# Plain float32 attention scores with a bias row for heads 8 to 11 of an attention, gate and spatial-mixing kernel

## The chip, the core and the metric

The kernel runs on one core of one Trainium2 chip. The metric is the device time of one execution in microseconds (us). The core's engines work side by side, each through its own list of instructions in order: PE (TensorE, matmuls; its weight loads are listed as PEld), DVE (VectorE), ACT (ScalarE), POOL (GpSimd) and SP (SyncE, which here only issues DMAs). An instruction that waits holds up all that stands behind it on its engine.

## What is computed

Three layers follow each other for a batch of 4 with 576 positions. The first is causal attention with 8 heads of width 64 (32 heads over the batch), whose scores get a bias from running sums of `s`; the second is a gated linear layer whose gate is a causal convolution over five positions; the third is a mixing layer over positions.

```python
scores = scale * np.matmul(q, k.transpose(0, 1, 3, 2))
s_pos = np.maximum(s, 0.0)
cum = np.cumsum(s_pos, axis=-1)
bias = -(cum[:, :, :, None] - cum[:, :, None, :])
scores = np.where(causal, -1000000000.0, scores + np.minimum(bias, 0.0))
scores = scores - np.max(scores, axis=-1, keepdims=True)
attn = np.exp(scores)
attn = attn / (np.sum(attn, axis=-1, keepdims=True) + 1e-09)
...
return np.matmul(attn, v).astype(np.float32)
...
gate = 1.0 / (1.0 + np.exp(-gate_pre))
val = x @ w_val
return (gate * val @ w_out).astype(np.float32)
...
h = np.maximum(x @ w_in, 0.0)
u, v = (h[..., :d_ff // 2], h[..., d_ff // 2:])
v_n = (v - mu) / np.sqrt(var + 1e-06)
v_s = np.einsum('ts,bsd->btd', w_spatial, v_n) + b_spatial[None, :, None]
gated = u * v_s
return (gated @ w_out).astype(np.float32)
```

The part of the bias that depends on the row alone drops out of the softmax, so a head's scores are q times k, plus the running sum of the column, under the causal mask.

## The kernel before

The main loop runs over heads, `w` from 0 to 32. In round `w` the kernel emits the scores of head `w` (`scores`), the transposes of head `w - 1` (`transposes`), and in every second round the product with v for a pair of heads (`pv`) and their convolution (`conv`). A head's queries are cut into five tiles of 64, 128, 128, 128 and 128 rows; their causal widths in keys are 64, 192, 320, 448 and 576, and the last is done as two pieces of 288 columns. That makes six score products of 1600 columns together per head.

There are two ways to a head's scores, chosen by `h < NATIVE`:

- **Native** (heads 1 to 7; head 0 likewise, but adds the sums by a second matmul): `load` brings q and k in float32 to 64 partitions of a buffer `raw` (two of them, `raw0_66` and `raw1_67` in the listings below, used in turn), and a row of running sums to partition 64, where the q side has ones. `scores` then issues one float32 matmul per product (L214), straight from `raw`.
- **Split** (heads 8 to 31): `load` brings q and k twice, to 128 partitions. `prep` rounds them on ACT (`hi_of`, L72, tile `qk`), subtracts on DVE (`lo_of`, L79, tiles `qk` and `kd`), and copies the rounded q by DMA to `cn` (L171); the running sums, split in two rows, come by DMA to `kd` (L169). `scores` then issues two matmuls in the rounded format per product (L216 and L217).

`load(w + 2)` is issued at the start of round `w` when `w >= NATIVE` and at its end otherwise. A native head's `raw` buffer is read by PE until the head's last score product; a split head's buffer is free once `prep` has read it.

Between these pieces `more` takes steps from a queue of other work and lets them in by an amount `n_g` per round: while heads run, the queue folds two weight matrices into one (`fold_prep`, `fold`: L420 to L422 from `wih`, `wil`, `wo_h`, results `wch` and `wcl`), prepares weights that arrive as float64 (`weight_prep`: load L380, ACT L382 and L388, DVE, a split, store L412 to `wv_d` or `wo_d`), and does the later layers of the batch before (`mixing_a`, `mixing_b`). In `mixing_a` the gate needs a sigmoid over the finished convolution `z` (L514), for which ACT loads another table and then returns to that of the exponential. `mixing_b` begins with four products read out by ACT at L544 and a fifth read out at L549, and its PSUM tiles `psm` are two in number, so a third product waits until the first is read out.

The row sums of a pair of heads travel from ACT to DRAM (L247, `r_d`) and back to a broadcast tile `R` (L253); DVE's L305 multiplies the pair's output by it.

The order in which each engine's instructions stand is not fixed by hand: the framework schedules the emitted pieces with a timeline of its own, so a change in one place can move others.

Of the kernel before, what the change touches and what calls it, by code (L numbers as in the profile page):

```python
# [13 lines left out]
PSUM = bass.MemoryType.PSUM  # L14

NEG = -1.0e30
NATIVE = 8


F64_LOW = 2.0 ** (896 // 8 - 127 + 16)  # L20
# [4 lines left out]
def tile_stickbreak_attention_moe(  # L25
# [52 lines left out]
    def lo_of(eng, out_, in_, hi):  # L78
        eng.tensor_tensor(out=out_, in0=in_, in1=f(hi), op=ALU.subtract)  # L79
# [51 lines left out]
    cum_d = dram.tile([NH, 2, S], F32, name="cum_d")  # L131
    one_d = dram.tile([max(NATIVE, 1), S], F32, name="one_d")

# [5 lines left out]
    def load(h, cum=None):  # L139
        if h >= NH:  # L140
            return
        raw[h] = r = RAW[h % 2]
        src = qk2[h].rearrange("p (t s) -> p t s", t=2)
        if h < NATIVE:
            SY.dma_start(r[0:64], src[0:64])
            if h:
                if h < 3:
                    SY.dma_start(r[64:65, 0, :], f(cn[0][64:65]))
                SY.dma_start(r[64:65, 1, :], one_d[h:h + 1] if cum is None else cum[h:h + 1])
        else:  # L150
            SY.dma_start(r, src)
        vraw[h] = early.tile([128, 5, D], F32, tag="vraw", name="vraw", bufs=4)
        SY.dma_start(vraw[h], vp[h].rearrange("p (c d) -> p c d", c=5))
# [3 lines left out]
    def prep(h):  # L157
# [3 lines left out]
        r = raw.pop(h)  # L161
        if h < NATIVE:
            st[h] = r
# [27 lines left out]
    def scores(h, tiles):  # L191
        if h >= NATIVE:
            qa, kb, qc, kd = st[h]
# [7 lines left out]
        for i in tiles:  # L201
            q0, m, e = QS[i], QM[i], QE[i]
            spans = [(0, e)] if e <= 512 else [(0, HS), (HS, e)]
            for a, b in spans:
                if pst is None or o + b - a > 512 or len(spans) > 1:
                    pst = room("s", "pss", h)
                    o = 0
                if h < NATIVE:
                    r = st[h]
# [128 lines left out]
    lo_of(V, cl, cum, ch)  # L338
    if NATIVE:
        load(0, cum)  # L340
# [446 lines left out]
```

## Time and profile before

| | |
|---|---|
| time, median of 3 runs | 522.56 us (522.26 to 524.95) |
| span of the profiled execution, from its first to its last instruction | 522.8 us |
| mean granted TensorE clock, as a share of full speed | 0.977 |
| PE busy | 491.1 us, 94% of the span |
| PEld busy | 414.2 us, 79% |
| ACT busy | 340.7 us, 65% |
| DVE busy | 316.6 us, 61% |
| POOL busy | 125.9 us, 24% |

The profiled execution's own time is given only as its span. Shares are averages over stages with different limits; matmuls are pipelined and their ends are modelled, so "busy" on PE is not the same as work at full pace.

### The profile page before, as it was taken

To read this page: it belongs to the slowest core of one execution; us is meant where nothing else is said; L and a number is where in the kernel's file an instruction comes from. 1 tells how busy PE (TensorE), PEld (TensorE's weight loads), DVE (VectorE), ACT (ScalarE), POOL (GpSimd) and SP (SyncE) were. 2 spreads that over 40 slices of the span, in tenths; PEclk is the share of its full clock that TensorE was granted. 3 is DMA by queue.
4 is the path that set the end of the run, shared out by engine and by line. 5 is a ranking of instruction groups with operands and counts; after the bars stand their busy time and mean duration, and the time that the engine had idled before them with its cause. 6 is when DMAs were issued, how large, how long until landed. Compare 5 with 4: busy or idle time off the path is not lost.

```text
span 522.8 us, 9120 instructions
## 1 busy us (share of the span) xinstructions
PE 491.1 (94%) x3206; PEld 414.2 (79%) x3206; DVE 316.6 (61%) x836; ACT 340.7 (65%) x819; POOL 125.9 (24%) x166
## 2 busy tenths in 40 slices
PE   7988888889997999989999999999998999999997
PEld 4555555769786898978958889888878888998997
DVE  5697999597986784834648456743876525025120
ACT  3797897697848783875738647795869644224322
POOL 5131221014452013201333013003233013145140
PEclk8699999998998999999999999999998999999999
DMA  6746964455572452266521302666510061700002
GB/s 180 240 134 212 300 245 147 119 168 189 175 242 92 132 184 82 64 216 204 178 83 39 127 27 84 192 211 178 169 32 15 26 209 70 241 1 1 1 3 89
DMA packets 28335, 69.27 MB, mean 132 GB/s; under 512 B 4033, under 2 KB 12385, under 8 KB 28289
## 3 DMA queue, kind: packets, MB, share of 16 engines
q1 hardware_dynamic: 23360, 63.88, 39.3%
q10 hardware_dynamic: 4928, 4.80, 2.7%
q8 instruction: 25, 0.41, 0.3%
q14 instruction: 22, 0.17, 0.1%
HBM read 55.96 MB, written 9.16 MB: 125 GB/s over the span
## 4 chain that ended last, share of the span: by engine, by line
PE 64%; DMA 12%; ACT 10%; DVE 9%; issue 3%; POOL 1%; SPq 1%; ACTq 0%; DVEq 0%; POOLq 0%
PE psm L420 12%; PE psm L422 11%; PE psm L421 11%; PE pst L276 6%; PE pso L300 5%; PE psm L592 3%; PE psm L594 3%; PE psm L593 3%; PE pss L216 3%; ACT p L229 2%; DVE z L317 2%; PE pss L217 2%; DMA R<-r_d 2%; DMA wo_d<-wr 2%; DVE p L224 1%
## 5 line engine op out<-in xcount | busy, mean ns | idle before, releaser
L229 ACT ACTIVATE p<-p,nm 64x64 f32<-64x64 f32 (+4 forms) x160 | 88.7, 556 | 15.2 <-DVE nm L224 14.7
L276 PE MATMUL pst<-ident,p 128*128 128x128 f32 x480 | 81.6, 279 | 6.2 <-ACT p L229 3.6
L224 DVE CUSTOM_DVE_ANT_0 p<-pss,mask 64x64 f32<-64x64 f32 (+4 forms) x160 | 63.9, 419 | 25.8 <-PE pss L217 19.2
L277 ACT ACTIVATE pt<-pst 128x512 f32<-128x512 f32 (+1 forms) x128 | 61.5, 497 | 26.3 <-PE psq L300 15.6
L276 PEld LDWEIGHTS pst<-ident,p 128*128 128x128 f32 x480 | 59.1, 142 | 17.4 <-ACT p L229 4.6
L317 DVE SCALAR_TENSOR_TENSOR z<-x,cw,z 128x575 f32<-128x575 f32 (+1 forms) x64 | 57.6, 901 | 6.2 <-ACT z L314 5.8
L79 POOL TENSOR_TENSOR y<-gt,y 128x288 fp32r<-128x288 f32 x32 | 27.4, 861 | 106.7 <-ACT y L72 106.7
L79 POOL TENSOR_TENSOR g<-gt,g 128x288 fp32r<-128x288 f32 x32 | 28.7, 901 | 101.1 <-ACT g L72 101.0
L300 PE MATMUL pso<-pt,vraw 128*64 128x448 f32 (+3 forms) x320 | 46.8, 418 | 0.6 <-ACT pt L277 0.6
L216 PE MATMUL pss<-qk 128*64 128x64 f32 (+1 forms) x144 | 44.9, 330 | 0.6 <-DVE qk L79 0.5
L217 PE MATMUL pss<-kd,cn 66*64 66x64 f32 (+1 forms) x144 | 41.9, 296 | 0.0
L300 PEld LDWEIGHTS pso<-pt,vraw 128*64 128x64 f32 x320 | 22.0, 136 | 24.9 <-issue 18.0
L420 PE MATMUL psm<-g,wch 128*128 128x288 f32 x128 | 39.7, 312 | 0.2 <-DVE v L550 0.2
L497 DVE TENSOR_TENSOR gt<-psm,u 128x288 f32<-128x288 f32 x32 | 14.4, 456 | 40.6 <-PE psm L596 30.4
L592 PE MATMUL psm<-wsh,vh 128*128 128x288 f32 x128 | 38.4, 305 | 0.6 <-DVE gt L497 0.6
L421 PE MATMUL psm<-g,wcl 128*128 128x288 f32 x128 | 38.7, 302 | 0.0
L422 PE MATMUL psm<-g,wch 128*128 128x288 f32 x128 | 38.3, 301 | 0.0
L593 PE MATMUL psm<-wsh,vl 128*128 128x288 f32 x128 | 37.5, 298 | 0.0
L594 PE MATMUL psm<-wsl,vh 128*128 128x288 f32 x128 | 37.4, 297 | 0.0
L497 DVE TENSOR_TENSOR gt<-psm,z 128x288 f32<-128x288 f32 x32 | 14.3, 451 | 34.7 <-PE psm L422 32.6
L214 PE MATMUL pss<-raw 128*128 128x288 f32 (+4 forms) x84 | 28.3, 438 | 6.3 <-DVE nm L224 6.2
L72 ACT ACTIVATE y<-gt 128x288 fp32r<-128x288 f32 x32 | 14.0, 442 | 29.2 <-DVE gt L497 29.2
(171 smaller groups left out, 1358.1 us busy)
## 6 DMA issues: line engine op xcount, KB each, us to landing
raw<-in_qk SPq DMA_DIRECT2D x24, 576.0 KB
wv<-wv_d SPq DMA_DIRECT2D x12, 512.0 KB
wv<-wo_d SPq DMA_DIRECT2D x12, 512.0 KB
vraw<-in_vp SPq DMA_DIRECT2D x32, 160.0 KB
R<-r_d SPq DMA_DIRECT2D x32, 160.0 KB
out<-ot ACTq DMA_DIRECT2D x32, 144.0 KB
cn<-qk SPq DMA_DIRECT2D x24, 144.0 KB
wr<-in_w_in SPq DMA_DIRECT2D x5, 512.0 KB
```

What stands on the lines that cost most here:

```text
L79: eng.tensor_tensor(out=out_, in0=in_, in1=f(hi), op=ALU.subtract)
L216: T.matmul(pst[0:m, o:o + b - a], qa[:, q0:q0 + m], kb[:, a:b], start=True, stop=False)
L224: LAST["V"] = V.tensor_tensor_reduce(out=p[i][0:m, a:b], in0=src, in1=mask[0:m, o:o + b - a], scale=-0.125, scalar=3.0e38 if a == 0 else n ...
L229: A.activation(p[i][0:m, 0:e], p[i][0:m, 0:e], AF.Exp, bias=nm[0:m, i:i + 1], scale=-1.0, accum_out=sm[h // 2 % 2][0:m, h % 2, i:i + 1])
L276: T.transpose(pt[:, o - o0:o - o0 + 128], p[i][:, c * 128:(c + 1) * 128], ident[:, r:r + 128])
L277: A.activation(PT[h][:, o0:end], pt[:, 0:end - o0], AF.Copy)
L300: m = T.matmul(po[64 * j:64 * j + 64, a - q0:q1 - q0], vs[j][:, c, :], pts[j][:, o:o + q1 - a], start=c == cs[0], stop=c == cs[-1])
L317: V.scalar_tensor_tensor(out=z[:, d:], in0=x[:, :S - d], scalar=cw[:, p, k:k + 1], in1=z[:, d:], op0=ALU.mult, op1=ALU.add)
L420: T.matmul(pt, ah, bh, start=j == 0, stop=False)
L421: T.matmul(pt, al, bh, start=False, stop=False)
L422: T.matmul(pt, ah, bl, start=False, stop=j == n - 1)
L592: T.matmul(o, vh[c][:, cs], wsh[:, c, hs[hf]], start=c == 0, stop=False)
```

## The change

One number changes. Heads 8 to 11 go the native way.

```diff
-NATIVE = 8
+NATIVE = 12
```

What follows from it in the code: for these four heads `prep` only hands `raw` on, so two ACT roundings, two DVE subtractions and two DMAs (`cn`, `kd`) per head are not issued; `load` brings 64 partitions in place of 128, and one more row from `one_d` (which holds 12 rows in place of 8); the six products of a head are one float32 matmul each in place of a pair; and `load(10)` to `load(13)` are issued at the end of rounds 8 to 11 and not at their start. On PE, the order from head 23 on is the same as before.

Three places show how the order moves. Numbers behind an underscore tell buffers and tiles apart, and those of the tiles differ between the two programs for the same tile.

The first is ACT around the end of head 8 (`p04`) and the beginning of head 9 (`p10`, `p11`). `rt` are the row sums of heads 6 and 7. Before:

```order
L277 ACTIVATE pt_820<-pst_874 128x512
L229 ACTIVATE p03_109,sm0_102<-p03_109,nm_810 128x448
L72 ACTIVATE qk_996<-raw0_66 128x576 x2
L229 ACTIVATE p04_110,sm0_102<-p04_110,nm_810 128x576
L229 ACTIVATE p10_117,sm0_102<-p10_117,nm_934 64x64
L229 ACTIVATE p11_118,sm0_102<-p11_118,nm_934 128x192
L246 ACTIVATE rt_832<-psr_830 10x128
L247 DMA r_d_131<-rt_832 10x128
```

The same place in the changed kernel:

```order
L229 ACTIVATE p03_109,sm0_102<-p03_109,nm_802 128x448
L257 ACTIVATE wch_63<-psm_899 128x512
L246 ACTIVATE rt_822<-psr_820 10x128
L277 ACTIVATE pt_810<-pst_855 128x512
L229 ACTIVATE p04_110,sm0_102<-p04_110,nm_802 128x576
L247 DMA r_d_131<-rt_822 10x128
L229 ACTIVATE p10_117,sm0_102<-p10_117,nm_914 64x64
L229 ACTIVATE p11_118,sm0_102<-p11_118,nm_914 128x192
```

The DMA of the row sums moves ahead of head 9's first two exponentials, and head 10's two roundings, which stood ahead of it, are gone.

The second is ACT ahead of `mixing_b`'s fifth read-out (L549). `wr` is the last of the four chunks of `w_out2` to be prepared, which arrives by DMA. Before:

```order
L72 ACTIVATE vh0_1346<-v_1263 128x512
L544 ACTIVATE v_1421<-psm_1420 128x512
L72 ACTIVATE vh1_1416<-v_1351 128x512
L544 ACTIVATE v_1473<-psm_1472 128x512
L277 ACTIVATE pt_1684<-pst_1688 128x512
L277 ACTIVATE pt_1684<-pst_1721 128x512
L229 ACTIVATE p12_119,sm0_102<-p12_119,nm_1674 128x320
L388 ACTIVATE wr_1932<-wr_1932 128x512
L549 ACTIVATE v_1559<-psm_1558 64x512
```

The same place in the changed kernel:

```order
L544 ACTIVATE v_1372<-psm_1371 128x512
L72 ACTIVATE vh0_1299<-v_1221 128x512
L72 ACTIVATE vh1_1367<-v_1304 128x512
L277 ACTIVATE pt_1460<-pst_1464 128x512
L544 ACTIVATE v_1425<-psm_1424 128x512
L277 ACTIVATE pt_1460<-pst_1498 128x512
L388 ACTIVATE wr_1884<-wr_1884 128x512
L229 ACTIVATE p03_109,sm0_102<-p03_109,nm_1450 128x448
L549 ACTIVATE v_1511<-psm_1510 64x512
```

L388, which waits for the chunk's DMA, stands close ahead of L549 in both. The chunk's buffer is the one that the second chunk's store has to leave; from the second chunk's rounding on ACT to this L388 there stand 12 instructions before the change, two of them L544, and 16 after it, four of them L544.

The third is SP's queue around the load of head 13. Before, it stands among heads 10 to 12's preparation, well ahead of all chunks of `w_out2`:

```order
L153 DMA vraw_932<-in_vp 128x320
L169 DMA kd1_99<-cum_d_134 2x576
L171 DMA cn1_97<-qk_1170 64x576
L151 DMA raw1_67<-in_qk2 128x1152
L169 DMA kd0_98<-cum_d_134 2x576
L253 DMA R_1232<-r_d_131 64x640
L482 DMA wv_1146<-wv_d_132 128x1024
```

In the changed kernel the load of head 13 is the first of the two `raw1_67` here, behind the store of the first chunk of `w_out2`:

```order
L380 DMA wr_1762<-in_w_out2 128x1024
L447 DMA wsr_1731<-in_wsT 128x576
L153 DMA vraw_1217<-in_vp 128x320
L153 DMA vraw_1402<-in_vp 128x320
L412 DMA wo_d_133<-wr_1719 128x1024
L151 DMA raw1_67<-in_qk2 128x1152
L380 DMA wr_1820<-in_w_out2 128x1024
L482 DMA wv_2293<-wo_d_133 128x1024
L171 DMA cn1_97<-qk_1491 64x576
```

Its buffer is now one that head 11's last score product on PE has to leave, and the load of the third chunk, `wr_1820`, stands behind it. On ACT, head 13's roundings (`qk_1491`), the second chunk's rounding, the third chunk's L388 and the first L544 follow each other directly in the changed kernel.

## Rows read from the trace of the kernel before

**Rows 1.** The page's busy time of each engine in us, share, instructions.

```profile
PE 491.1 (94%) x3206; PEld 414.2 (79%) x3206; DVE 316.6 (61%) x836; ACT 340.7 (65%) x819; POOL 125.9 (24%) x166
```

**Rows 2.** Busy time by stretch of the span; the first column is the stretch.

```profile
core 0: us, PE busy (x) PEld busy (x) DVE busy (x) ACT busy (x) POOL busy (x), PEclk, DMA share, GB/s
78.10:99.40 21.30, 18.95 (x115) 14.35 (x116) 15.90 (x41) 15.03 (x39) 1.72 (x1) 1.00 0.46 146
99.40:118.40 19.00, 14.79 (x102) 11.34 (x101) 17.86 (x49) 17.27 (x37) 2.46 (x2) 1.00 0.51 151
118.40:121.90 3.50, 3.50 (x17) 3.50 (x16) 1.10 (x3) 3.50 (x10) 1.57 (x2) 0.51 0.84 318
121.90:159.40 37.50, 34.55 (x214) 29.29 (x212) 31.60 (x73) 25.32 (x62) 16.76 (x19) 1.00 0.59 186
159.40:162.80 3.40, 3.32 (x8) 2.65 (x9) 2.78 (x10) 3.38 (x8) 2.74 (x3) 0.50 0.00 0
162.80:296.10 133.30, 131.08 (x915) 115.45 (x914) 84.26 (x222) 91.26 (x225) 28.54 (x33) 1.00 0.41 128
```

**Rows 3.** Timeline of PE: start, us, what; in brackets idle before, releaser.

```profile
84.04 0.74 PE L422 MATMUL psm<-wil,wo_h 128*128 128x512 f32 x2 [0.58 <-DVE wil L79]
...
87.36 0.33 PE L276 MATMUL pst<-ident,p 128*128 128x128 f32 x1 [1.05 <-ACT pt L277]
...
89.36 0.97 PE L300 MATMUL pso<-pt,vraw 128*64 128x448 f32 x4 [0.62 <-ACT pt L277]
...
101.96 0.50 PE L420 MATMUL psm<-wih,wo_h 128*128 128x512 f32 x1 [1.94 <-DVE wcl L79]
...
116.82 0.87 PE L276 MATMUL pst<-ident,p 128*128 128x128 f32 x6 [1.76 <-ACT p L229]
...
159.48 0.80 PE L420 MATMUL psm<-wih,wo_h 128*128 128x512 f32 x1 [2.73 <-DVE v L550]
```

**Rows 4.** Timeline of PE where it does not wait: the pace of products.

```profile
74.00 1.14 PE L214 MATMUL pss<-raw 128*128 128x288 f32 x4
74.97 0.27 PE L276 MATMUL pst<-ident,p 128*128 128x128 f32 x1
...
97.62 0.40 PE L422 MATMUL psm<-wil,wo_h 128*128 128x512 f32 x1
97.86 0.29 PE L216 MATMUL pss<-qk 128*128 128x288 f32 x1
...
98.39 0.27 PE L276 MATMUL pst<-ident,p 128*128 128x128 f32 x1
```

**Rows 5.** Groups by line and shape: count, then busy us, mean ns, idle before.

```profile
L72 ACT ACTIVATE qk<-raw 128x576 fp32r<-128x576 f32 x48 | 30.1, 676 | 3.7 <-PE pss L216 3.5 <-DMA raw<-in_qk 0.2
...
L79 DVE TENSOR_TENSOR kd<-raw,qk 64x576 fp32r<-64x576 f32 x24 | 19.6, 818 | 0.5
...
L79 DVE TENSOR_TENSOR qk<-raw,qk 64x576 fp32r<-64x576 f32 x24 | 18.8, 783 | 6.0 <-ACT qk L72 5.3
```

**Rows 6.** Timelines of ACT's queue, SP's queue and DVE: heads 6 and 7's row sums.

```profile
92.87 0.28 ACTq L247 DMA_DIRECT2D r_d<-rt  x1
...
96.39 1.11 SPq L253 DMA_DIRECT2D R<-r_d  x2
...
100.42 0.62 DVE L305 TENSOR_TENSOR x<-pso,R 128x448 f32<-128x448 f32 x1 [1.63 <-DMA R<-r_d]
```

**Rows 7.** The chain that ended last: start, us, what; the end of weight preparation.

```profile
145.68 8.11 DMA wo_d<-wr
...
153.81 3.55 DMA wr<-in_w_out
```

**Rows 8.** Timeline of ACT: the sigmoid of the first batch, and the fourth chunk's L388.

```profile
112.46 2.13 ACT L514 ACTIVATE z<-z 128x2304 f32<-128x2304 f32 x1
...
157.44 0.65 ACT L388 ACTIVATE wr<-wr 128x512 int32<-128x512 uint32 x1 [3.43 <-DMA wr<-in_w_out]
```

## The prediction

> **What bounds the kernel now.** I read the page's busy time first, then cut the span into stretches, then went through PE's timeline for the places where it waits, and last followed the longest of these waits back through the chain. The page puts PE at 94% of the span and its weight loads at 79% [rows 1]; no other engine is near. But this is an average. By stretch [rows 2], PE's idle time is the length less the busy time: 21.30 - 18.95 = 2.35 us from 78.1 to 99.4 (heads 8 and 9), 19.00 - 14.79 = 4.21 us from 99.4 to 118.4, 37.50 - 34.55 = 2.95 us from 121.9 to 159.4, together 9.5 us; and then only 133.30 - 131.08 = 2.2 us in the next 133 us. So the heads that the change touches run in the one part where PE still waits for others, and behind it PE is simply full. In the two short stretches at 118.4 and 159.4 the granted clock is 0.51 and 0.50, that is 1.2 GHz in place of 2.4; right before them PE had waited 1.76 us (the wait at 116.82) and 2.73 us [rows 3]. Work of 3.5 and 3.4 us at half clock loses half of it: 1.75 and 1.7 us.
>
> The waits themselves [rows 3] are for ACT and DVE being late: 0.58, 1.05 and 0.62 us in head 8; 1.94 us at 101.96 for DVE's L79, which stood behind a product that waited for the broadcast row sums [rows 6]; 1.76 us at 116.82 for ACT, which had done the sigmoid's 2.13 us and the table loads around it [rows 8]; and 2.73 us at 159.48 for DVE's L550, which hangs on ACT's L549, which stood behind an L388 that waited 3.43 us for its weights [rows 8].
>
> PE's busy time also hides short gaps, since a matmul's modelled end overlaps the next one. Weight loads show them better: they are busy 115.45 / 133.30 = 87% of the full stretch, and (14.35 + 11.34 + 29.29) / 77.80 = 71% of the three stretches that wait [rows 2]. At 87% these 54.98 us of loads would take 63.5 us, so there are 14.3 us to spare, 4.8 us more than the idle time shows. The Trainium skill, in "Perfetto Trace Analysis", section Identifying the Most-Contended Engine, calls matmul busy time a poor measure and gives weight-load occupancy as a better one. By that rule the 94% would be no ground to charge each added PE microsecond to the span; by the busy figure alone it would be. The trace agrees with the rule as far as 71% against 87% goes.
>
> **The change part by part.**
>
> *More PE work.* Two native products of 288 columns took 74.97 - 74.00 = 0.97 us in their four records, 0.485 us each. Two split pairs of 288 columns took 98.39 - 97.86 = 0.53 us, 0.265 us each [rows 4]. The difference is 0.22 us per 288 columns; a head has 1600 columns, so 0.22 x 1600 / 288 = 1.22 us, and four heads cost **+4.9 us** of PE time. If it fell only into waits it would cost 0; I charge all of it and count the waits that go as gains of their own.
>
> *Less ACT and DVE work.* Eight roundings at 676 ns are 5.4 us of ACT; four pairs of subtractions at 818 and 783 ns are 6.4 us of DVE [rows 5]. Neither is worth its length: both engines are waited for only at the places above. What is late next is what counts:
>
> - Head 8's three waits, 2.25 us. Ahead of them both engines lose heads 8 and 9's conversion, 2.7 us of ACT and 3.2 us of DVE by the same means. More than the waits; but PE's own scores take 1.2 us longer there and ACT has other work. I take **-2.0 us** (between 0 and 2.25).
> - The wait of 1.94 us at 101.96. The DMA of the row sums was issued on ACT at 92.87, the broadcast on SP at 96.39, and DVE's product started at 100.42 after 1.63 us of idling [rows 6]. In the new order that DMA stands ahead of head 9's first two exponentials, and two roundings (1.35 us) ahead of it are gone [rows 5]; with head 8's 2 us this is earlier by more than 1.94 us, and SP has no `cn` copy left ahead of the broadcast. I take **-1.9 us** (0 to 1.94).
> - The sigmoid's wait of 1.76 us and the half clock behind it, 1.75 us. The sigmoid, its two table loads and what they hold up stay. It moves to an earlier place among ACT's instructions, and PE can do no more mixing than two PSUM tiles until it is done. I take 0 (0 to -3.5).
> - The wait of 2.73 us at 159.48 and its 1.7 us of half clock. The chunk's load waits for the second chunk's store; these took 8.11 and 3.55 us [rows 7]. This time runs from the second chunk's rounding. Before, 12 instructions of ACT cover it, two of them L544; afterwards 16, four of them L544. An L544 comes after twelve products of 512 columns, 97.86 - 97.62 = 0.24 us each [rows 4], so 2.9 us of PE; two more cover 5.8 us against a wait of 3.43 us [rows 8]. I leave 0.5 us of the wait and take **-3.9 us** (0 to -4.4).
> - Short gaps, 4.8 us at most by the weight loads: with ACT and DVE lighter by 5 to 6 us some go; a fifth, **-1.0 us** (0 to -4.8).
>
> *A new wait.* Head 13's load now needs `raw1` from head 11's last product, and the third chunk's load stands behind it on SP. On ACT, head 13's roundings and the third chunk's L388 stand right ahead of the first L544, and PE can do two products of four weight chunks each (24 matmuls, 5.8 us) and some transposes before it needs that L544. The load is 576 KB; at the 3.55 us that 512 KB took [rows 7] it is 4.0 us, and with two roundings (1.35 us) some 5.4 us are gone before the split and the L388. If the third chunk's load lands beside it, PE waits next to nothing, 0.3 us; if it follows, 3.55 us more, 3.9 us. ACT's wait then also holds head 12's exponentials. I take **+1.0 us**, nearer the low end, since the DMA engines are half idle there (share 0.59) [rows 2] and two loads can run side by side.
>
> *At nothing:* the halves of the four loads that fall away, the four `cn` copies and the `kd` rows, and the four new rows of running sums. They ran beside other work, at a DMA share of about half [rows 2]; no PE wait above ends on one of them.
>
> Sum: 4.9 - 2.0 - 1.9 - 3.9 - 1.0 + 1.0 = **-2.9 us**, on the profiled 522.8 us a span of 519.9 us. That execution stands 0.2 us from the median, 522.56 us, so I forecast a time of **519.7 us**.
>
> **The rivals.**
>
> 1. *The sigmoid's wait goes too.* With PE's list heavier there, and the convolution done sooner, the stall may shrink under other work and the clock stay at 2.4 GHz: 3.5 us more, and with half of the short gaps 1.4 more, 514.8 us. For it: the broadcast that fed the last convolution comes earlier. Against: ACT's stall of 2.13 us and two table loads is the same length. The Trainium skill, in "TensorE: Matmul & The Clock Gate", section What's actually happening, says the slow clock is the default state that activity releases; by that rule a fuller PE would keep 2.4 GHz. The trace agrees in that both half-clock stretches follow PE's longer waits, but a wait of 1.94 us was followed by none.
> 2. *The last wait stays.* The weights come when the DMAs bring them, and the mixing that needs them comes earlier. Then the 3.9 us are not got back: 519.7 + 3.9 = 523.6 us, no change. For it: 8.11 us of store and 3.55 us of load in a row [rows 7], which no compute engine shortens.
> 3. *Slower: PE's work counts in full and the new wait takes the gain's place.* If head 13's load and the third chunk's follow each other, PE stands at the third product with the full 3.9 us, and drops to half clock as at 159.4, 1.7 us: 519.7 + 2.9 + 1.7 = 524.3 us; with the last wait kept as well, 528.2 us; with a part of it, 526. It decides the sign when the new wait and its clock cost more than 2.9 + 1.0 = 3.9 us. For it: nothing but those loads stands between head 11's last product and the L544. Against: the share of idle DMA time.
>
> That the change does not do what it says is not to be expected: in the new lists the four heads' pairs are gone.
>
> **How the numbers follow.** My forecast, with 516.5 to 521.5 us as its own range, gets 0.45; the first rival 0.18, the second 0.19, the third 0.18. A change of 0.5%, 2.6 us, is about what a measurement of this kernel can tell from none; so faster means below 519.95 us, slower above 525.2 us. Faster: 0.6 of the forecast's 0.45 and all of the first rival's 0.18, 0.45. Same: the other 0.18 of the forecast, 0.16 of the second rival, 0.06 of the third, 0.40. Slower: 0.15. The range runs from 514.0 us (most of the first rival) to 526.0 us (most of the third).
>
> **What would show it.** Right: PE starts head 10 about 1 to 2 us sooner than 99.4, no wait near 1.94 us for L79 in head 9, and no half clock ahead of L549's product; the wait of DVE for `R` there is gone. PE's added time shows as four L214 heads at about 2.7 us each. Wrong: an L388 wait of over 3 us ahead of L544 or L549, with PE idle and a half-clock stretch behind it; or a sigmoid that stalls PE for longer than 1.8 us; or new PE waits after 163 us, where there were none of weight.

## The result and the profile after

The changed kernel took 528.93 us (median of 4 runs, 525.65 to 530.26) against 522.41 us for the kernel before in the same comparison (522.1 to 524.95, 4 runs): a ratio of 1.0102, with a 95% interval of 1.0057 to 1.0147. It is slower by 1.0%, where 0.5% faster was forecast, and the range ended 2.9 us below the measured time.

A trace shows one execution, and executions of one program differ: in the runs beside the first experiment the kernel before took 518.15 us at a mean granted clock of 0.993 and 524.77 us at 0.971. A wait of 2 us in one trace is therefore a lead to be tried, not yet a part of the median.

The page's busy times after (engine, busy us, share of the span, instructions), which answer to [rows 1]; the span is 527.7 us:

```profile
PE 500.4 (95%) x3206; PEld 417.4 (79%) x3206; DVE 312.2 (59%) x828; ACT 335.6 (64%) x811; POOL 122.7 (23%) x166
```

ACT and DVE did 5.1 and 4.4 us less work (5.4 and 6.4 were forecast), and PE was busy 9.3 us longer. To see where, the span is cut at two points at which PE has the same work behind it in both kernels: head 8's first score and head 23's (from which on PE's order is the same). The windows of before are:

```profile
78.10:296.10 218.00, 206.20 (x1362) 176.59 (x1363) 153.50 (x394) 155.76 (x375) 53.79 (x60) 0.98 0.46 143
296.10:522.80 226.70, 218.16 (x1540) 198.18 (x1537) 101.77 (x258) 123.60 (x286) 51.70 (x68) 0.99 0.30 93
```

The same two pieces after (from:to, length, then busy us of PE, PEld, DVE, ACT, POOL, granted clock, DMA share, GB/s), and the three short stretches of half clock that lie in the first of them:

```profile
76.40:302.60 226.20, 215.53 (x1361) 179.28 (x1361) 149.55 (x386) 151.67 (x368) 50.73 (x60) 0.98 0.45 134
302.60:527.70 225.10, 217.10 (x1540) 196.89 (x1537) 101.36 (x258) 123.31 (x286) 51.59 (x68) 1.00 0.30 93
...
137.20:140.60 3.40, 3.20 (x8) 2.53 (x9) 3.03 (x12) 2.73 (x11) 0.27 (x2) 0.51 0.86 286
195.30:198.70 3.40, 2.90 (x12) 2.90 (x13) 3.07 (x8) 2.71 (x8) 0.00 (x0) 0.50 0.16 36
236.20:239.60 3.40, 3.07 (x13) 3.07 (x14) 0.67 (x4) 3.40 (x13) 0.00 (x0) 0.50 0.33 116
```

The middle piece grew from 218.0 to 226.2 us, by 8.2; the other two shrank by 1.7 and 1.6 (the last because a stretch of half clock that stood there before is not there after, see the last section). In the middle piece PE's busy time grew by 215.53 - 206.20 = 9.3 us, but its idle time fell only from 11.8 to 10.7 us. Of the 9.3 us, 1.2 are clock: PE was busy for 3.20 + 2.90 + 3.07 = 9.17 us at half clock, of which half is lost, 4.6 us, against half of 3.50 + 3.32, 3.4 us, before [rows 2]. So PE got its dearer matmuls, as forecast, and some 3 us more, but the idle time that was to pay for them is still there.

It is not the same idle time. PE's waits of over 0.5 us in that piece after (start, busy, instruction, in brackets the idle time before it and what ended it; to be held against [rows 3]):

```profile
84.93 0.44 PE L276 MATMUL pst<-ident,p 128*128 128x128 f32 x2 [0.85 <-ACT pt L277]
...
107.82 0.40 PE L420 MATMUL psm<-xvh,wv 128*128 128x288 f32 x1 [1.17 <-DVE wcl L79]
...
120.79 0.37 PE L420 MATMUL psm<-xvh,wv 128*128 128x288 f32 x1 [1.08 <-DMA wv<-wv_d]
...
128.17 0.50 PE L420 MATMUL psm<-wch,g 128*128 128x512 f32 x1 [0.57 <-DVE gt L497]
...
137.40 0.80 PE L420 MATMUL psm<-wch,g 128*128 128x512 f32 x1 [1.91 <-ACT v L544]
...
195.80 0.61 PE L592 MATMUL psm<-wsh,vh 128*128 128x288 f32 x1 [2.52 <-ACT u L580]
...
236.53 0.69 PE L276 MATMUL pst<-ident,p 128*128 128x128 f32 x2 [2.23 <-ACT p L229]
```

One wait of before in that piece the prediction did not name, its timeline of PE has it as:

```profile
231.76 0.37 PE L420 MATMUL psm<-y,wv 128*128 128x288 f32 x1 [1.76 <-DMA wv<-wo_d]
```

This one is gone after, those at 101.96, 116.82 and 159.48 are gone, and of head 8's three there is one of 0.85 us left. Together 1.94 + 1.76 + 2.73 + (2.25 - 0.85) + 1.76 = 9.6 us of idle time went. The six other rows bring 9.5 us back. Three of them are long, and a half-clock stretch stands at each.

ACT shows what PE waited for. Its timeline ahead of each of the three:

```profile
134.04 1.26 ACT L72 ACTIVATE qk<-raw 128x576 fp32r<-128x576 f32 x2 [1.55 <-DMA raw<-in_qk]
135.21 0.61 ACT L72 ACTIVATE wr<-wa 128x512 fp32r<-128x512 f32 x1
136.19 0.67 ACT L388 ACTIVATE wr<-wr 128x512 int32<-128x512 uint32 x1 [0.37 <-DMA wr<-in_w_out]
136.76 1.07 ACT L544 ACTIVATE v<-psm 128x512 f32<-128x512 f32 x2
...
194.77 0.68 ACT L72 ACTIVATE ws<-wsr 128x576 fp32r<-128x576 f32 x1 [1.39 <-DMA wsr<-in_wsT]
195.36 0.39 ACT L580 ACTIVATE u<-psm 128x288 f32<-128x288 f32 x1
...
230.87 1.28 ACT L514 ACT_TABLE_LOAD   x1
232.17 2.13 ACT L514 ACTIVATE z<-z 128x2304 f32<-128x2304 f32 x1
234.31 1.28 ACT L229 ACT_TABLE_LOAD   x1
235.61 0.78 ACT L229 ACTIVATE p<-p,nm 128x576 f32<-128x576 f32 x1
```

The first is the new wait of the prediction, in the place and order described there: head 13's roundings wait 1.55 us for their load, `wr` 0.37 us for its chunk, and PE's two `psm` tiles wait for L544 behind them. The second has the same form at another place: the read-out L580, whose product PE had finished by 193.3, stands behind a rounding of the spatial weights (`ws`) that waits for a DMA. This pair is not new: it stands so before the change too, where the rounding also waits and PE does not:

```profile
191.62 0.69 ACT L72 ACTIVATE ws<-wsr 128x576 fp32r<-128x576 f32 x1 [0.85 <-DMA wsr<-in_wsT]
192.22 0.69 ACT L580 ACTIVATE u<-psm 128x288 f32<-128x288 f32 x2
```

The third is the sigmoid of the second batch, 4.7 us of ACT between one exponential and the next, with PE's transposes waiting for the latter.

### The profile page after: what moved, and what is told of

It reads as the page before. It is cut to its first block, busy times and chain, and to the rows that moved or that the text cites. A ratio compares the mean times of both kernels' runs of the same rounds, so it can differ in the third digit from the quotient of the medians.

```text
span 527.7 us, 9087 instructions
## 1 busy us (share of the span) xinstructions
PE 500.4 (95%) x3206; PEld 417.4 (79%) x3206; DVE 312.2 (59%) x828; ACT 335.6 (64%) x811; POOL 122.7 (23%) x166
## 3 DMA queue, kind: packets, MB, share of 16 engines
HBM read 54.77 MB, written 9.17 MB: 121 GB/s over the span
## 4 chain that ended last, share of the span: by engine, by line
PE 66%; ACT 12%; DMA 11%; DVE 7%; issue 2%; POOL 1%; SPq 1%; ACTq 0%; POOLq 0%; DVEq 0%
PE psm L420 11%; PE psm L422 11%; PE psm L421 11%; PE pst L276 7%; PE pso L300 7%; PE psm L592 3%; PE psm L594 3%; PE psm L593 3%; ACT p L229 3%; PE pss L216 2%; PE pss L217 2%; DMA wr<-in_w_in 2%; DVE z L317 2%; PE pss L214 1%; DMA wv_d<-wg 1%
## 5 line engine op out<-in xcount | busy, mean ns | idle before, releaser
L276 PEld LDWEIGHTS pst<-ident,p 128*128 128x128 f32 x480 | 60.5, 145 | 19.3 <-ACT p L229 5.2
L79 POOL TENSOR_TENSOR g<-gt,g 128x288 fp32r<-128x288 f32 x32 | 27.4, 860 | 137.3 <-ACT g L72 137.3
L317 DVE SCALAR_TENSOR_TENSOR z<-x,cw,z 128x575 f32<-128x575 f32 (+1 forms) x64 | 55.4, 865 | 6.6 <-ACT z L314 6.0
L79 POOL TENSOR_TENSOR y<-gt,y 128x288 fp32r<-128x288 f32 x32 | 27.0, 847 | 114.0 <-ACT y L72 114.0
L300 PE MATMUL pso<-pt,vraw 128*64 128x448 f32 (+3 forms) x320 | 49.9, 420 | 0.0
L214 PE MATMUL pss<-raw 128*64 128x64 f32 (+3 forms) x132 | 44.2, 438 | 5.1 <-DVE nm L224 4.9
L420 PE MATMUL psm<-g,wch 128*128 128x288 f32 x128 | 38.7, 306 | 0.2 <-ACT v L544 0.2
L422 PE MATMUL psm<-g,wch 128*128 128x288 f32 x128 | 37.7, 300 | 0.0
L216 PE MATMUL pss<-qk 128*64 128x64 f32 (+2 forms) x120 | 36.7, 325 | 0.4 <-DVE nm L224 0.3
L217 PE MATMUL pss<-kd,cn 66*64 66x64 f32 (+2 forms) x120 | 34.8, 296 | 0.0
L214 PEld LDWEIGHTS pss<-raw 128*128 128x128 f32 (+1 forms) x132 | 20.8, 192 | 15.6 <-DVE nm L224 10.0
```

What stands on the lines that cost most here:

```text
L214: T.matmul(pst[0:m, o:o + b - a], r[:, 0, q0:q0 + m], r[:, 1, a:b], start=True, stop=True)
L276: T.transpose(pt[:, o - o0:o - o0 + 128], p[i][:, c * 128:(c + 1) * 128], ident[:, r:r + 128])
L300: m = T.matmul(po[64 * j:64 * j + 64, a - q0:q1 - q0], vs[j][:, c, :], pts[j][:, o:o + q1 - a], start=c == cs[0], stop=c == cs[-1])
L317: V.scalar_tensor_tensor(out=z[:, d:], in0=x[:, :S - d], scalar=cw[:, p, k:k + 1], in1=z[:, d:], op0=ALU.mult, op1=ALU.add)
L420: T.matmul(pt, ah, bh, start=j == 0, stop=False)
L422: T.matmul(pt, ah, bl, start=False, stop=j == n - 1)
```

## The experiments

Two theories. **P**: the dearer matmuls count in full wherever PE is near full, and the relief of ACT and DVE pays little back. **O**: the order in which the framework puts the instructions decides; what was gained comes back as waits where a read-out stands behind an instruction that waits for a DMA. Ratios are to the kernel before (allowance 11.5) on the same chip, with 95% intervals. The allowance is the second number of the list `n_g`, which says how much other work is let in per round in rounds 9 to 12; it moves instructions and adds or removes none.

**Price alone** (`e1_price_alone`). All preparation stays, only the matmuls of heads 8 to 11 are the dearer ones.

```diff
-T.matmul(pst[...], qa[:, q0:q0 + m], kb[:, a:b], start=True, stop=False)
-T.matmul(pst[...], qc[0:KD, q0:q0 + m], kd[0:KD, a:b], start=False, stop=True)
+T.matmul(pst[...], f(qa[:, q0:q0 + m]), f(kb[:, a:b]), start=True, stop=True)   # h < 12
```

> The kernel before, with heads 8 to 11 still prepared on ACT and DVE and by DMA as split heads, but each of their score products issued as one plain float32 matmul on the rounded operands (the second half-product and the bias are left out, so the values of these heads differ). It adds the price on PE, +4.9 us, and removes nothing. Theory P (PE's added work stays in the time, because PE is full behind this part): 527 us, against 522.4 us of before. Theory O (the loss comes from three new waits that the new order brings, at 137.4, 195.8 and 236.5 us in the changed kernel, and PE's work alone falls into waits that are there anyway): 522 to 524 us.

Measured: 530.67 us, 1.0154 (1.0111 to 1.0197). That is 8 us, more than the 4.9 us of the matmuls and more than either theory named. In its trace PE also waits 3.28 us for an exponential at 108.15, with half clock behind it; but that execution was the quickest of the six (527.42 us), and PE's idle time in it is 29.1 us against 31.7 before, so the trace does not show where the rest of the 8 us lies.

**Relief alone** (`e2_no_price`). The changed kernel, but in heads 8 to 11 three eighths of the columns in float32 and the rest as a product of zeros in the rounded format.

```diff
-T.matmul(pst[...], r[:, 0, q0:q0 + m], r[:, 1, a:b], start=True, stop=True)
+n = (b - a) // 8 * 3
+T.matmul(pst[0:m, o:o + n], r[:, 0, q0:q0 + m], r[:, 1, a:a + n], start=True, stop=True)
+T.matmul(pst[0:m, o + n:o + b - a], wz[:, 0:m], wz[:, 0:b - a - n], start=True, stop=True)
```

> The changed kernel, with the products of heads 8 to 11 cut: the first 3/8 of the columns as a float32 matmul, the rest as one matmul of zeros in the rounded format (these columns' scores are left out). That is 3/8 x 4 + 5/8 = 2.1 passes per column, against 2 of the split pair and 4 of the plain float32: PE's price is nearly gone, the preparation of four heads stays away. Theory P: 528.9 - 4.6 = 524.3 us, or below before if the relief of ACT and DVE is worth anything by itself. Theory O: within 1 us of the changed kernel, 528 to 529 us, as its waits stay.

Measured: 523.03 us, 1.0026 (0.9997 to 1.0055). With 5 us less of ACT and 7 us less of DVE and nearly no price on PE (its busy time is 0.9 us above that of before), nothing is gained. Theory P's 524.3 us was nearer than theory O's 528 to 529. PE's waits stand elsewhere, 2.39 us at 85.68 and 3.08 us at 190.62, the latter for L580 again (line numbers are five higher here):

```profile
85.68 0.77 PE L281 MATMUL pst<-ident,p 128*128 128x128 f32 x5 [2.39 <-ACT pt L282]
...
190.62 0.40 PE L597 MATMUL psm<-wsh,vh 128*128 128x288 f32 x1 [3.08 <-ACT u L585]
```

**A buffer of their own for heads 10 and 11** (`e3_own_buffer`), so that head 13's load need not wait for head 11's products.

```diff
-raw[h] = r = RAW[h % 2]
+if h in (10, 11):
+    r = raw[h] = f(early.tile([128, 2, S], F32R, tag="qk", name="rawq", bufs=2))
+else:
+    raw[h] = r = RAW[h % 2]
...
-if w >= NATIVE:
+if w >= 10:
```

The products of these two heads then read 65 partitions in place of 128; one record of 288 columns took 419 ns on average in this trace, and 433 ns in the changed kernel.

> The changed kernel, with q and k of heads 10 and 11 loaded into the two buffers of the split heads' rounded operands, which are free until head 12 is prepared. The loads of heads 12 and 13 then wait for heads 8 and 9 and are issued at the start of rounds 10 and 11. Theory O: the wait of PE at 137.4 us, 1.91 us, and its half clock, 1.7 us, go: 528.9 - 3.6 = 525.3 us. Theory P: they go there, but come back at a later wait, since the time is PE's work plus what the chain of weight loads holds up: 527 to 529 us.

Measured: 527.81 us, 1.0101 (1.0066 to 1.0136). The wait at 137 is gone from the trace and the time is nearly the same, as theory P had it and not theory O (525.3 us); 2.20 us at 193.25 (L580) and 2.38 us at 234.25 (sigmoid) stayed, and 1.90 us at 110.68 came.

**The kernel before, with another order** (`e4_before_12`).

```diff
-n_g = [3, 11.5, 10.0, 7.6, 6.0][...]
+n_g = [3, 12.0, 10.0, 7.6, 6.0][...]
```

> The kernel before, with the allowance of queued work in rounds 9 to 12 at 12.0 in place of 11.5. No work is added or removed; only the order of the instructions shifts. It gives the size of what an order alone does to the time. Theory P: within 1.5 us of 522.4 us. Theory O: orders by themselves are worth several us, so it may well lie 3 us or more away, 519 to 527 us.

Measured: 523.77 us, 1.0033 (1.0002 to 1.0064). This other order is worth 0.3%, less than the 3 us that theory O named.

**Price alone, late** (`e5_price_late`): the edit of the first experiment on heads 24 to 27 (`24 <= h < 28`).

> As e1, the price on PE alone, but on heads 24 to 27, where PE hardly waits, in place of heads 8 to 11 (their second half-product and bias are left out). Theory P (added PE work stays in the time wherever it stands): +4.9 us on before, 527 us, and within 2 us of e1's cost. Rival W (PE's waits around heads 8 to 11 absorb part of the price there): the full 4.9 us here and clearly less in e1; since e1 cost some 8 us, W would have to be dropped if this is 5 us or less.

Measured: 523.73 us, 0.9996 (0.9963 to 1.003). The same four heads' worth of dearer matmuls cost nothing here, where theory P and its rival W had both put the full price. The window in which they run, before:

```profile
320.00:400.00 80.00, 76.06 (x528) 66.64 (x527) 50.05 (x136) 61.65 (x143) 16.36 (x22) 0.98 0.45 134
```

and with the late price:

```profile
320.00:400.00 80.00, 79.43 (x533) 67.43 (x533) 49.37 (x134) 61.72 (x139) 16.56 (x22) 1.00 0.45 134
```

PE is busy 3.4 us longer, and 1.7 us of half clock are gone, so the price is there in full: about 5.1 us. Its idle time fell from 3.9 to 0.6 us. A price can be real and still cost nothing, as long as there are waits for it to fall into and none take their place.

**Relief for eight heads** (`e6_relief_8`): heads 8 to 15 native, with the cut products of the second experiment.

```diff
-NATIVE = 8
+NATIVE = 16
```

> As e2, but for eight heads, 8 to 15: no preparation on ACT, DVE and by DMA, and PE's price nearly gone (most columns' scores of these heads are left out). Twice the relief of e2. Theory P, with PE's work and the later chain as the bound: relief is worth nothing here, within 1.5 us of before. Rival R (relief is worth about a microsecond per head, and e2 lost it to an unlucky order): 4 us or more below before, 518 us or less.

Measured: 527.86 us, 1.0106 (1.0062 to 1.015). Twice the relief, nearly no price, and slower. Neither theory P nor rival R has room for this, and in the trace the loss is not idle time either: PE is busy 5.4 us longer than before and idle 2.8 us less.

**The spatial weights' rounding on GpSimd** (`e7_ws_on_pool`): the changed kernel, so that L580 no longer stands behind it on ACT.

```diff
-hi_of(A, L["ws1"], t)
+hi_of(G, L["ws1"], t)
```

> The changed kernel, with one rounding of the position weights (tile ws1, the one on which ACT waited 1.39 us for its DMA ahead of the read-out L580 that PE waited for at 195.8 us) on GpSimd in place of ACT. Theory G (what the relief gained was given back at single later waits, this one the longest: 2.52 us and 1.7 us of half clock): 528.9 - 4.2 = 524.7 us. Theory P: the wait moves to the next late thing, 527 to 529 us.

Measured: 527.03 us, 1.0115 (1.0066 to 1.0165). The wait for L580 fell to 0.23 us; the sigmoid's, 2.00 us at 232.20, stayed. The 524.7 us of theory G did not come, and a gain over the changed kernel can't be told from none. The wait for L544, which this edit does not touch, is 0.78 us in this trace and has no half clock behind it; what follows from that is said with the cause below.

**Six native heads** (`e8_native_6`): the change made the other way.

```diff
-NATIVE = 8
+NATIVE = 6
```

> The other way: NATIVE = 6, so heads 6 and 7 are split too. PE loses 2 x 1.22 = 2.4 us of work, ACT and DVE gain 2.7 and 3.2 us at a place where ACT is busy all the time (20 of 20 us). Theory P, price in full everywhere: 520 us. Rival A (ahead of head 8 ACT and DVE are the bound, so there relief counts and PE's price does not): 524 to 526 us.

Measured: 529.21 us, 1.0131 (1.0096 to 1.0165). Slower in this direction too, against both forecasts. Though PE has less work, its busy time is 4.0 us above that of before and its idle time 1.4 us: at a mean granted clock of 0.967 against 0.977, the larger part of the loss shows as half clock.

**The changed kernel at 11.0 and 12.0** (`e9_after_11`, `e10_after_12`), **the kernel before at 11.0** (`e11_before_11`), **price alone at 12.0** (`e12_price_12`): the edit of the fourth experiment with these numbers.

> The changed kernel with the allowance of queued work in rounds 9 to 12 at 11.0 in place of 11.5. No work changes; PE's order is that of the changed kernel up to about head 13 and another one behind it. Theory P (PE's added work stays in the time whatever the order): 527 to 530 us. Theory O (the loss is what the changed kernel's later order gives back, at 195.8 and 236.5 us): another order may lie anywhere from 521 to 530 us, and a time under 525 us speaks for O.

Measured: 519.13 us, 0.9944 (0.9908 to 0.998).

> As e9 with 12.0: PE's order is that of the changed kernel up to about head 13 and a third one behind it. Theory P: 527 to 530 us. Theory O: away from 528.9 us by 3 us or more; under 525 us speaks for O.

Measured: 530.31 us, 1.0164 (1.0117 to 1.0211).

> The kernel before at 11.0. Both theories: theory P 521 to 524 us; theory O, if orders alone make several us, up to 528 us. With e4 it says whether the kernel before stands at a lucky order.

Measured: 519.77 us, 0.996 (0.9921 to 1.0).

> The price alone of e1 (heads 8 to 11 prepared and still scored by one plain float32 matmul each; second half-product and bias left out) at 12.0. Theory P: as e1, 528 to 532 us. Theory O: e1's 530.7 us was its order; 522 to 527 us here.

Measured: 535.27 us, 1.0265 (1.0216 to 1.0314).

The first is what theory O allowed and theory P did not. The second lies 0.3 us above P's range and is not the 3 us away that O asked for. The third is below P's range, the fourth above the ranges of both.

With the same work, order alone takes the changed kernel from 519.13 to 530.31 us. At 11.0 ACT reads out ahead of head 13's roundings:

```profile
133.07 0.58 ACT L544 ACTIVATE v<-psm 128x512 f32<-128x512 f32 x1
133.55 0.59 ACT L277 ACTIVATE pt<-pst 128x512 f32<-128x512 f32 x1
135.06 1.26 ACT L72 ACTIVATE qk<-raw 128x576 fp32r<-128x576 f32 x2 [0.92 <-DMA raw<-in_qk]
...
188.20 0.67 ACT L72 ACTIVATE ws<-wsr 128x576 fp32r<-128x576 f32 x1
188.77 1.06 ACT L277 ACTIVATE pt<-pst 128x512 f32<-128x512 f32 x2
189.72 0.70 ACT L580 ACTIVATE u<-psm 128x288 f32<-128x288 f32 x2
```

The rounding still waits 0.92 us for the load, but PE waits for nothing that stands behind it; and `ws` no longer waits at all. The trace has no PE wait of over 1.1 us after 122 us. At 12.0 it is the reverse, on ACT:

```profile
132.92 1.26 ACT L72 ACTIVATE qk<-raw 128x576 fp32r<-128x576 f32 x2 [1.07 <-DMA raw<-in_qk]
134.09 0.61 ACT L72 ACTIVATE wr<-wa 128x512 fp32r<-128x512 f32 x1
137.13 0.66 ACT L388 ACTIVATE wr<-wr 128x512 int32<-128x512 uint32 x1 [2.43 <-DMA wr<-in_w_out]
137.69 1.06 ACT L544 ACTIVATE v<-psm 128x512 f32<-128x512 f32 x2
```

and PE waited 3.65 us for this L544.

**Price alone and relief alone at other allowances** (`e13_price_11`, `e14_no_price_11`, `e15_no_price_12`): the edits of the first two experiments together with that of the fourth.

> The changed kernel's matmuls alone, with the work of preparation and the loads of before kept, at an allowance of 11.0 in rounds 9 to 12; before at this allowance took 519.8 us and the changed kernel 519.1. Theory P (the dearer matmuls always count in full, and what is relieved on ACT and DVE pays them back): 519.8 + 4.9 = 524.7 us or more, ratio to before about 1.004. Theory O (the order of the instructions behind head 13 makes the time, matmuls and relief next to nothing): within 1.5 us of 519.8, ratio about 0.995.

Measured: 528.44 us, 1.0105 (1.0056 to 1.0155).

> The changed kernel at an allowance of 11.0 with its twelve heads native, but heads 8 to 11 with 3/8 of the columns in float32 and the rest as a product of zeros in the rounded format, so that PE's time is near that of before (the scores of these heads are not the reference's). Theory P: the relief without the price, 519.1 - 4.9 = 514.2 us, ratio about 0.984. Theory O: 519 us, as the changed kernel at 11.0, ratio about 0.994.

Measured: 519.25 us, 0.9942 (0.9908 to 0.9976).

> The same cut products at an allowance of 12.0, where before took 523.8 us and the changed kernel 530.3. Theory P: 530.3 - 4.9 = 525.4 us or less, ratio about 1.006; if the relief is worth something, under 523.8. Theory O: anything from 519 to 530 us, with a sum of waits and half clock that answers to it.

Measured: 528.40 us, 1.0112 (1.0072 to 1.0151).

The ratios side by side:

| allowance | before | relief alone | price alone | both (the change) |
|---|---|---|---|---|
| 11.0 | 0.9960 | 0.9942 | 1.0105 | 0.9944 |
| 11.5 | 1 | 1.0026 | 1.0154 | 1.0102 |
| 12.0 | 1.0033 | 1.0112 | 1.0265 | 1.0164 |

The first of these three fell to theory P (524.7 us or more), the second to theory O (519 us); the third missed theory P's 525.4 us, while theory O had left it open.

Neither theory holds as it was put. With the preparation kept, the price costs 1.45 to 2.3 points at every allowance, 7.6 to 12 us. With the preparation gone, taking it away again brings 0.0 points at 11.0, 0.8 at 11.5 and 0.5 at 12.0. Relief by itself makes the kernel 0.2 points faster, 0.3 slower and 0.8 slower. Each ratio is good to 0.3 to 0.5 points, so of these last six only the 0.8 are clear of noise, and those barely. So the two don't add: the relief is worth something only as room for the price, and how much of the price it takes up, all of it or a part, differs with the order.

**Both waits taken away at once** (`e16_buffer_and_ws`): the edits of the third and the seventh experiment in one kernel, at 11.5.

> The changed kernel with two of its new waits taken away at once: heads 10 and 11 in buffers of their own, loaded early, so that no rounding of head 13 waits ahead of the read-out, and the rounding of the spatial weights on GpSimd, so that no read-out stands behind it. If these waits are the loss (their 1.91 and 2.52 us and 1.7 us of half clock behind each, 7.8 us), 528.9 - 7.8 = 521 us, ratio about 0.998. If PE is merely late by the dearer matmuls and waits come back elsewhere (as with each edit alone, 527.8 and 527.0): 526 to 528 us, ratio about 1.009.

Measured: 523.04 us, 1.0013 (0.9982 to 1.0045). The loss is gone; the time lies between the two forecasts, nearer to the first. PE's waits in the same piece, head 8 to head 23 (line numbers are up to four higher than above):

```profile
110.71 0.66 PE L280 MATMUL pst<-ident,p 128*128 128x128 f32 x4 [1.90 <-ACT p L233]
...
191.24 0.40 PE L599 MATMUL psm<-ws,s 128*128 128x288 f32 x1 [0.65 <-POOL ws L74]
194.83 0.42 PE L220 MATMUL pss<-qk 128*128 128x320 f32 x1 [0.54 <-DVE nm L228]
231.07 0.66 PE L280 MATMUL pst<-ident,p 128*128 128x128 f32 x4 [2.29 <-ACT p L233]
```

and its windows:

```profile
78.80:297.30 218.50, 212.53 (x1371) 178.41 (x1371) 148.12 (x390) 151.89 (x367) 52.28 (x61) 0.99 0.44 135
297.30:523.00 225.70, 218.10 (x1539) 198.39 (x1537) 101.81 (x258) 123.66 (x286) 51.61 (x68) 0.99 0.30 93
```

PE is busy 6.3 us longer than before in this piece and idle 5.8 us less (5.97 against 11.8 us), so the piece is as long as before, 218.5 against 218.0 us. The sigmoid's wait and its half clock are still there.

## Why the prediction was wrong

- **The account of the middle piece**, in the prediction's own terms: price 4.9 us, more clock 1.2 us, other busy time of PE 3.2 us, idle time -1.1 us, together 8.2 us. The forecast for it was the price less 8.8 us of waits, clock and short gaps, plus 1.0 us for a new wait.
- **The price** was right in kind and size. In the trace after, four L214 records of PE start at 125.91 and its next instruction at 126.88: 0.97 us for two products of 288 columns, as costed, and the late price showed 5.1 us for four heads against 4.9.
- **The short gaps** went the other way. They were booked at -1.0 us; PE's busy time without the clock's 1.2 us grew by 8.1 us, 3.2 us more than the price. From which rows these come I can't say, since modelled ends hide short gaps.
- **The named waits** went, as forecast: L79's in head 9, the one for L549 with its half clock, and most of head 8's. The sigmoid's first wait, put at zero, went too, so the first rival's mechanism came about (3.5 us), without its time.
- **The new wait** came where and how it was described, and was mis-sized: +1.0 us against 1.91 us and 1.6 us of half clock behind it, 3.5 us. The low end was chosen because the DMA engines were half idle. That share, 0.59 [rows 2], is the mean of 37.5 us; while the load of head 13 was under way, from its issue at 128.25 to ACT's start at 134.04, it was 0.91, and the load took 5.8 us where 4.0 were costed:

```profile
128.20:134.00 5.80, 5.80 (x27) 4.67 (x28) 5.75 (x13) 4.30 (x10) 3.54 (x3) 1.00 0.91 287
```

  The third rival had named this wait and its half clock. That its 528.2 us lies near the measured time is luck: it reaches that figure by keeping the last wait, which went.
- **The step that failed** is "behind it PE is simply full", by which the waits that go were booked as gains for good, and nothing was charged after 163 us. The row itself had 2.2 us of idle time there, of which one wait was 1.76 us, so "none of weight" was not so. After the change PE waited at 195.80 (2.52 us, clock 0.50 behind it) and at 236.53 (2.23 us, clock 0.50), in place of that one without loss of clock. The prediction named "new PE waits after 163 us" as what would prove it wrong, and gave them no term and no share of the chance. Of 9.6 us of idle time that went, 9.5 came back. Why they came there is shown in part only: the `ws` rounding stood ahead of L580 before as well, and waited 0.85 us without holding up PE.
- **What is shown of the cause:** the order of the same work is worth 11 us in the changed kernel, and at 11.0 the change costs nothing. Which waits make up the loss at 11.5 is shown in part. The edits against the two waits left 1.0101 and 1.0115 one by one, and 1.0013 together, and between the piece of the changed kernel and that with both edits lie 4.7 us of idle time and two of three half-clock stretches. But in the trace of the seventh experiment both waits are short already. ACT's order over the 20 us ahead of this L544, and PE's order up to 190 us, are there those of the changed kernel, where the wait was 1.91 us; so the order around a wait does not fix its length. And the piece from head 8 to head 23 still takes 221.4 us, 3.4 more than before:

```profile
135.47 0.50 PE L420 MATMUL psm<-wch,g 128*128 128x512 f32 x1 [0.78 <-ACT v L544]
...
77.00:298.40 221.40, 214.21 (x1361) 177.17 (x1361) 147.38 (x386) 151.27 (x367) 52.26 (x61) 0.99 0.44 136
```

  So these two waits are not shown to be the whole loss. The kernel with both edits also has an order of its own and was timed at one allowance alone; that it stands at a lucky order is a rival that no run here rules out. That the sigmoid's remaining wait is what keeps it from being faster is argued, not tried.
- **The base** was slightly off: in every profiled execution after, the time stands 1.8 us above the span (529.46 and 527.7 us; 524.82 and 523.0), and the prediction set a span against a median of times. By this the traced execution of before took some 524.6 us (an estimate), 2.2 us above its median. It changes no sign.
- What stays open: which order a given change will get. Relief alone was slower at 12.0 than before at 12.0 (1.0112 and 1.0033) for less work on ACT and DVE, and I know no row of before from which that could have been read.

The Trainium skill, in "Perfetto Trace Analysis", section Identifying the Most-Contended Engine, prefers weight-load occupancy to matmul busy time. The trace agrees: from head 8 to head 23 PE's busy share rose from 94.6% to 95.3% while the kernel got slower, and the weight loads' share fell from 176.59 / 218.0 = 81.0% to 179.28 / 226.2 = 79.3%; with both waits away it is 81.7%.

The best version measured is the change at an allowance of 11.0, 519.13 us, below both kernels; but the kernel before at 11.0 (519.77 us) can't be told from it. What gain there is goes with the order, not with the change, and the interval of the kernel before at 11.0 reaches up to 1.0.

## What to carry to other kernels

Where an engine is near full, cost a change as price less the idle time that it fills, and then ask of every wait that goes whether the instructions that caused it, a DMA-fed rounding ahead of a read-out on an in-order engine, still exist; if so the wait may have moved, and the new order must be read for all such pairs, not only near the edit. Where a scheduler sets the order, time the change at two or three neighbouring settings of it before judging: here the setting moved the same work by 2%, the change itself by -0.2 to +1.3% at equal settings. And take suspected waits away together as well as one by one, and look in each trace whether the wait that was left alone is still there: here it was short as well in one of them.

## What was not expected of the hardware

A PE wait of nearly the same length was followed by half clock in one run and not in another. The plainest case lies behind head 23, where PE's order is the same before and after: ahead of the same transposes PE waited 1.26 us before and 1.27 us after, and for the next 3.4 us the granted clock was 0.50 before (the first two rows) and 1.00 after.

```profile
394.95 0.48 PE L276 MATMUL pst<-ident,p 128*128 128x128 f32 x1 [1.26 <-ACT p L229]
394.90:398.30 3.40, 3.35 (x13) 3.04 (x14) 2.83 (x10) 3.38 (x7) 2.05 (x3) 0.50 0.00 0
...
400.95 0.33 PE L276 MATMUL pst<-ident,p 128*128 128x128 f32 x1 [1.27 <-ACT p L229]
400.90:404.30 3.40, 3.20 (x23) 3.01 (x24) 2.82 (x10) 3.38 (x7) 2.04 (x3) 1.00 0.01 2
```

Longer waits differ in the same way. The 1.90 us at 110.7 had a granted clock of 0.5 behind it for 3.4 us with heads 10 and 11 in a buffer of their own, and none when the spatial weights were moved as well; the 3.08 us at 190.62 with relief alone had none, the 2.52 us at 195.80 in the changed kernel had 3.4 us. The Trainium skill, in "TensorE: Matmul & The Clock Gate", section What's actually happening, has the slow clock as the default that activity releases; the traces agree in that every stretch of half clock behind head 8 in the changed kernel stood at the end of a wait of PE (1.91, 2.52 and 2.23 us), but the length of the wait alone does not tell which ones do.
